# A fused attention and two-MLP kernel: scores of k by halves, attention spread over the batch before, idle-time products, float narrowing shifted to ScalarE

## The chip, the cores and the metric

One Trainium2 chip, one core. The metric is the device time of one execution in microseconds, the median of several runs. In the profile PE is TensorE's matrix products, PEld its weight loads, DVE VectorE, ACT ScalarE, POOL GpSimd and SP SyncE, whose queue issues nearly all transfers.

## The reference

For 8 batches with 8 heads, 576 tokens and 64 features per head, 32 packing queries p per head gather the sequence, and the tokens q read the gathered result; the heads then form rows of 512 for two MLPs:

```python
p_packed = softmax(p @ k.T / 8) @ v          # 32 x 64 per head
out = softmax(q @ p_packed.T / 8) @ p_packed # 576 x 64 per head
x = out.transpose(0, 2, 1, 3).reshape(4608, 512)
h = x @ w_in                                 # 512 x 2048
x = where(h > 0, h, exp(min(h, 0)) - 1) @ w_out
h = x @ w_in2                                # 512 x 1024
solu = h * softmax(h)
ln = (solu - mean(solu)) / sqrt(var(solu) + 1e-6) * g_ln
out = ln @ w_out2
```

q, k, v and p come as 4-byte floats, the four weight matrices as 8-byte floats.

## The kernel before

**Narrowing.** The weights arrive as pairs of 32-bit words and are made 4-byte floats in 48 units of 128 x 512 (`narrow`, L94): 32 for the first MLP (`wi`, `wo`), 16 for the second (`wi2`, `wo2`). Per unit ScalarE scales the high word as a float (L105), VectorE shifts it left by 3 (L107), ORs in the low word shifted right by 29 (L109) and ORs in the sign (L113). Planner names: cvA, cvS, cvO, cvG.

**Exact products.** Every big product takes three passes over a high and a low part of each operand (`mm3`, L64 to L66). The second product of attention is folded into w_in: M = p_packed times a 64-row block of w_in (`m_mm`), four chunks c per batch, so the first MLP's h comes straight from the attention weights AT and M.

**Attention of a batch.** Two groups g of four heads run one after the other: `s1_mm` forms the scores of k with p laid out as block diagonals (`pt_bd`, zeros elsewhere), 8 instructions of 128 rows by 64 columns; maximum, exponential and division (`s1_max`, `s1_exp`, `s1_div`); a transpose, in batches 0 and 1 on TensorE (`t1_mm`), from batch 2 on by VectorE's 32 x 32 blocks and 16 copies into `a_sb` (`t1_blocks`, `t1_move`, L295); then `pp_mm` multiplies by v and `pp_blocks` (L319) or `pp_t` puts the result, transposed, into `ppT`. Then two halves of 288 tokens: `s2_mm` (scores of q, 16 instructions of 64 rows by 32 columns through `packed_mm`, L332), softmax over blocks of 32 on VectorE, with the exponential on ScalarE (`s2_tr` to `s2_back`, L349 to L377), and a split into AT.

**FFN steps.** 256 steps (batch, half, f), each 6 products for h (L64 to L66), two activations on ScalarE (L418, L419), a maximum on VectorE (L424), a cast (L431) and a subtraction (L434), and, three steps behind, 12 products into the accumulators. The first three halves are done by quarters of f, so that not all weights are needed at once.

**PSUM.** Eight banks: two double ones "acc", one double one "misc" (scores, transposes, pp, M, in turn), two for h.

**The order.** A planner, `order`, emits all nodes of the first part on TensorE, VectorE, ScalarE and SP. A node has an engine, an estimated time, what it needs, the buffers that it takes and frees, and perhaps a due time; of the nodes that can start within 0.3 us on an engine the one with the earliest latest start is emitted. FFN step n is due at `FIRST_US + STEP_US * n` (30.0 and 2.79); attention nodes have no due time of their own, only what follows from their users. `first` is the order of the first transfers on SP's queue; p of batch 0 goes by ScalarE's queue in two pieces, after `pt_bd` is cleared. The last part (`solu_ln` to `out_mm`), the second MLP, follows in an order written out by hand.

Of the kernel before, what the change touches and what calls it, by code (L numbers as in the profile page):

```python
# [34 lines left out]
def attention_mlp_kernel(ctx: ExitStack, tc: tile.TileContext, q, k, v, v_tail, p,  # L35
# [58 lines left out]
    def narrow(raw, name, dst=None):  # L94
# [125 lines left out]
    def load_v(b, g, tag=None):  # L220
        if tag is None:
            t = v_sb
        else:
# [4 lines left out]
        vt[b, g] = t

    def load_q(b, half, tag=None):  # L230
        if tag is None:
            t = work.tile([P, 4, HS], F32, tag="q", name=f"q{b}_{half}", bufs=1)
        else:
            t = slot(f"q{b}_{half}", [P, 4, 512], tag, F32)[:, :, 0:HS]
        sp.dma_start(out=t, in_=q[b, half])
        qt[b, half] = t

    def s1_mm(b, g, ps2=misc_ps):
        o = ps2(f"s1_{b}_{g}")
        kk = kt.pop((b, g))  # L240
        for kh in range(2):
            for j in range(2):
                pe.matmul(o[64 * j:64 * j + 64, kh, 0:HS], pt_bd[:, 2 * g + j, :],
                          kk[:, j, kh * HS:(kh + 1) * HS], start=True, stop=True)
        st["s1", g] = o

    def s1_max(b, g):
        nm = small.tile([P, 1], F32, tag="nm", name=f"nm{b}_{g}")
        dve.tensor_reduce(out=nm, in_=st["s1", g][:, :, 0:HS], axis=AX.XY, op=ALU.max, negate=True)
        dve.tensor_scalar(out=nm, in0=nm, scalar1=0.125, scalar2=None, op0=ALU.mult)  # L250
        st["nm", g] = nm

    def s1_exp(b, g):
        e = work.tile([P, S], F32, tag="at", name=f"e1_{b}_{g}", bufs=3)
        sm = small.tile([P, 1], F32, tag="sm", name=f"sm{b}_{g}")
        act.activation(e.rearrange("p (a c) -> p a c", a=2), st.pop(("s1", g))[:, :, 0:HS], AF.Exp,
                       scale=0.125, bias=st.pop(("nm", g)), accum_out=sm)
        st["e1", g] = e, sm

    def s1_div(b, g):  # L260
        e, sm = st["e1", g]
        r = small.tile([P, 1], F32, tag="r", name=f"r{b}_{g}")
        dve.tensor_scalar(out=sm, in0=sm, scalar1=1e-9, scalar2=None, op0=ALU.add)
        dve.reciprocal(r, sm)
        dve.tensor_scalar(out=e, in0=e, scalar1=r, scalar2=None, op0=ALU.mult)

    def t1_mm(b, g, ps2=misc_ps):
        e, _ = st.pop(("e1", g))
        o = ps2(f"t1_{b}_{g}")
# [3 lines left out]
        st["t1", g] = o  # L273

    def t1_a(b, g):
        act.copy(a_sb[:, 0:4].rearrange("p c n -> p (c n)"), st["t1", g][:, 0])

    def t1_b(b, g):
        dve.tensor_copy(a_sb[0:S - 4 * CH, 4], st["t1", g][0:S - 4 * CH, 1, 0:P])

    def t1_blocks(b, g):
        e, _ = st.pop(("e1", g))
        t = work.tile([P, S], F32, tag="at", name=f"eB{b}_{g}", bufs=3)
        dve.transpose(t, e)
        st["eB", g] = t.rearrange("p (c n) -> p c n", n=NP)

    def t1_move(b, g, h, eng):
        t = st["eB", g]
        for j in range(4):
            n = len(range(j, S // NP, 4))  # L290
            x, y = a_sb[j * NP:(j + 1) * NP, 0:n, h * NP:(h + 1) * NP], t[h * NP:(h + 1) * NP, j::4]
            if eng is act:
                act.copy(x, y)
            else:
                dve.tensor_copy(x, y)  # L295

    def pp_mm(b, g, ps2=misc_ps):


        o = ps2(f"pp{b}_{g}")  # L300
        vv = vt.pop((b, g))
        for u in range(2 if b < 2 else 0):
            for c in range(5):
# [731 lines left out]
```

## Time and profile before

| | |
|---|---|
| median of 3 runs | 1182.26 us (1179.63 to 1182.43) |
| the profiled execution | 1178.58 us, of which the span is 1176.8 us |
| TensorE busy | 1117.9 us (95%) |
| VectorE busy | 894.4 us (76%) |
| ScalarE busy | 718.6 us (61%) |
| GpSimd busy | 21.3 us (2%) |
| mean granted clock of TensorE | 0.987 |

Busy shares are averages over the whole span; the kernel has an opening, a stretch in which weights are narrowed beside the first steps, a long steady stretch, and the second MLP. Matrix products are pipelined, so their durations overlap, and the distance between two starts tells the rate. A line can belong to a helper.

### The profile page before, as it was taken

Reading aid. Unit: us, or ns where it says so; the run is one execution under the profiler, and the core shown is the slowest. Engines: PE = TensorE matmul, PEld = TensorE weight load, DVE = VectorE, ACT = ScalarE, POOL = GpSimd, SP = SyncE. Lnnn points to the kernel's source line nnn. Section 1 sums busy time; section 2 is a strip of 40 time slices with the busy share of each in tenths; the row PEclk is TensorE's granted clock in tenths of the full one; section 3 lists DMA queues with packets and bytes.
Section 4 is the critical chain, followed back from the end, with each engine's and each line's share of the span. In section 5 each row is a group of like instructions: output and inputs, shape, how many; then the busy total and the mean of one; then the engine's idle time right before and its main releaser. Section 6 shows DMA issues by size and latency. Waiting matters only on the chain.

```text
span 1176.8 us, 20606 instructions
## 1 busy us (share of the span) xinstructions
PE 1117.9 (95%) x7916; PEld 979.5 (83%) x7916; DVE 894.4 (76%) x2022; ACT 718.6 (61%) x1539; POOL 21.3 (2%) x45
## 2 busy tenths in 40 slices
PE   4699999899999999999999999999999999999997
PEld 2478889699799899899889889988888888888885
DVE  4999995858858868767877765478888788788774
ACT  2567765465465565565466465647766766766674
POOL 0000000000000000000000000000000000000000
PEclk7799999999999999999999999999999999999999
DMA  9837332213322412321422151611111111000000
GB/s 328 333 117 235 121 111 82 84 41 113 101 93 72 145 57 97 119 93 62 132 80 90 46 178 59 218 57 54 54 37 54 52 39 54 27 28 19 28 28 36
DMA packets 53554, 111.04 MB, mean 94 GB/s; under 512 B 8400, under 2 KB 27600, under 8 KB 51664
## 3 DMA queue, kind: packets, MB, share of 16 engines
q1 hardware_dynamic: 52912, 109.66, 27.5%
q8 instruction: 62, 1.02, 0.4%
q14 instruction: 36, 0.29, 0.1%
q10 hardware_dynamic: 544, 0.07, 0.0%
HBM read 77.14 MB, written 32.57 MB: 93 GB/s over the span
## 4 chain that ended last, share of the span: by engine, by line
PE 42%; DVE 31%; ACT 14%; issue 7%; DMA 4%; POOL 1%; SPq 0%; ACTq 0%; POOLq 0%; DVEq 0%
PE acc L64 8%; PE acc L66 8%; PE acc L65 8%; ACT lnX L542 6%; PE h L64 5%; PE h L65 5%; PE h L66 4%; DVE lnB L532 4%; DVE a_sb L295 2%; DVE ln L525 2%; PE m L332 2%; DVE z L517 2%; ACT h L520 2%; DVE lnT L151 2%; DVE nm L508 2%
## 5 line engine op out<-in xcount | busy, mean ns | idle before, releaser
L64 PE MATMUL acc<-ghi,wo 128*128 128x288 f32 x1024 | 308.6, 301 | 1.7 <-ACT x L471 0.7
L66 PE MATMUL acc<-glo,wo 128*128 128x288 f32 x1024 | 302.7, 296 | 1.4 <-DVE glo L434 1.4
L65 PE MATMUL acc<-ghi,wo 128*128 128x288 f32 x1024 | 302.2, 295 | 0.0
L64 PEld LDWEIGHTS acc<-ghi,wo 128*128 128x128 f32 x1024 | 191.9, 187 | 30.8 <-ACT fe L419 14.8
L66 PEld LDWEIGHTS acc<-glo,wo 128*128 128x128 f32 x1024 | 192.6, 188 | 2.6 <-DVE glo L434 2.0
L65 PEld LDWEIGHTS acc<-ghi,wo 128*128 128x128 f32 x1024 | 192.6, 188 | 0.0
L559 PE MATMUL o<-wo,lnT 128*128 128x512 f32 (+1 forms) x592 | 185.5, 386 | 5.6 <-ACT lnT L149 5.6
L424 DVE SCALAR_TENSOR_TENSOR fe<-fe,h 128x288 f32<-128x288 f32 x256 | 114.3, 452 | 88.6 <-ACT fe L419 86.0
L418 ACT ACTIVATE fe<-h 128x288 f32<-128x288 f32 x256 | 104.5, 408 | 118.2 <-PE h L66 92.8
L431 ACT CAST ghi<-fe 128x288 fp32r<-128x288 f32 x256 | 109.4, 431 | 105.2 <-DVE fe L424 104.4
L64 PE MATMUL h<-AT,M 128*128 128x288 f32 x512 | 156.0, 305 | 9.7 <-DVE fe L424 8.9
L542 ACT COPY lnX<-lnB 32x256 f32<-32x256 f32 x288 | 116.3, 404 | 78.0 <-DVE lnB L532 65.2
L65 PE MATMUL h<-AT,M 128*128 128x288 f32 x512 | 152.4, 298 | 0.9 <-DVE M L400 0.9
L66 PE MATMUL h<-AT,M 128*128 128x288 f32 x512 | 150.8, 294 | 0.0
L434 DVE TENSOR_TENSOR glo<-fe,ghi 128x288 fp32r<-128x288 f32 x256 | 114.5, 452 | 46.4 <-ACT ghi L431 42.8
L559 PEld LDWEIGHTS o<-wo,lnT 128*128 128x128 f32 x592 | 111.3, 190 | 28.3 <-ACT lnT L149 6.5
L64 PEld LDWEIGHTS h<-AT,M 128*128 128x128 f32 x512 | 96.6, 189 | 27.5 <-DVE fe L424 11.4
L419 ACT ACTIVATE fe<-fe 128x288 f32<-128x288 f32 x256 | 113.8, 445 | 8.0
L561 PE MATMUL o<-wo,lnT 128*128 128x512 f32 (+1 forms) x296 | 113.9, 386 | 0.0
L64 PE MATMUL h<-wi,x2hi 128*128 128x512 f32 x288 | 112.3, 390 | 1.4 <-ACT h L520 1.4
L65 PE MATMUL h<-wi,x2lo 128*128 128x512 f32 x288 | 112.1, 389 | 0.0
L66 PE MATMUL h<-wi,x2hi 128*128 128x512 f32 x288 | 112.0, 389 | 0.0
(98 smaller groups left out, 1581.8 us busy)
## 6 DMA issues: line engine op xcount, KB each, us to landing
k<-in_k SPq DMA_DIRECT2D x16, 576.0 KB, 3.9
q<-in_q SPq DMA_DIRECT2D x16, 576.0 KB, 3.9
x_dram<-x SPq DMA_DIRECT2D x32, 288.0 KB, 2.5
x2raw<-x_dram SPq DMA_DIRECT2D x9, 1024.0 KB, 5.5
out_x<-y SPq DMA_DIRECT2D x35, 256.0 KB, 2.0
raw_wi<-in_w_in SPq DMA_DIRECT2D x8, 1024.0 KB, 9.3
w_dram<-w SPq DMA_DIRECT2D x16, 512.0 KB, 2.7
v_sb<-in_v SPq DMA_DIRECT2D x14, 512.0 KB, 3.9
```

The lines of the kernel that those rows point to most:

```text
L64: pe.matmul(o, a[0], b[0], start=start, stop=False)
L65: pe.matmul(o, a[1], b[0], start=False, stop=False)
L66: pe.matmul(o, a[0], b[1], start=False, stop=stop)
L418: act.activation(e, o[:, 0:HS], AF.Relu, scale=-1.0)
L419: act.activation(e, e, AF.Exp, scale=-1.0)
L424: dve.scalar_tensor_tensor(out=e, in0=e, scalar=-1.0, in1=o[:, 0:HS], op0=ALU.add, op1=ALU.max)
L431: act.copy(ghi, e)
L434: dve.tensor_tensor(out=glo, in0=e, in1=ghi.bitcast(F32), op=ALU.subtract)
L532: dve.transpose(t, last.pop(("ln", i)))
L542: act.copy(x, y)
L559: pe.matmul(o, t[:, x, kk], w[:, 0, cs], start=x + kk == 0, stop=x == 1 and kk == 7)
L561: pe.matmul(o, t[:, 0, kk], w[:, 1, cs], start=False, stop=False)
```

## The change

In `narrow` the left shift moves into the first OR, and the top three bits of the low word are made as an integer by a ScalarE activation, in place (cvL in the place of cvS). The scores of k come in two halves w of 288 tokens for all eight heads, with p undoubled (`p_sb`) and the same product form as the scores of q (`heads_mm`, which is `packed_mm` with the weights as an argument); the two halves' maxima, sums and factors are joined (`s1_both`, `s1_scale`, `s1_fac`). `a_sb` holds both halves r of the heads, and one pp group of a batch follows for both. k, q and v share three single buffers of one size from batch 2 on, and v has no zero rows any more. Attention nodes from batch 2 on get due times (`by`) within the 32 steps of the batch before. The first transfers are reordered, p first on SP's queue. Where the planner sees TensorE idle ahead of the first h, products of a tile of ones are issued into a spare h bank, which nobody reads. Lines of the old code that go, printed above, are mostly left out here.

```diff
--- before.py
+++ after.py
@@ -100,14 +100,16 @@
...
         act.activation(t.bitcast(F32), raw[:, :, 1].bitcast(F32), AF.Copy, scale=2.0 ** -111)
         yield
-        dve.tensor_scalar(out=t, in0=t, scalar1=3, scalar2=None, op0=ALU.logical_shift_left)
+        act.activation(raw[:, :, 0], raw[:, :, 0], AF.Identity, scale=2.0 ** -29 * (1 - 2.0 ** -10), bias=under)
         yield
-        dve.scalar_tensor_tensor(out=t, in0=raw[:, :, 0], scalar=29, in1=t,
-                                 op0=ALU.logical_shift_right, op1=ALU.bitwise_or)
+        dve.scalar_tensor_tensor(out=t, in0=t, scalar=3, in1=raw[:, :, 0],
+                                 op0=ALU.logical_shift_left, op1=ALU.bitwise_or)
...
+    under = const.tile([P, 1], F32, name="under")
...
-    pt_bd = const.tile([P, 4, 2 * NP], F32, name="pt_bd")
-    a_sb = const.tile([P, 5, P], F32, name="a_sb")
-    v_sb = const.tile([P, 5, 4 * D], F32, name="v_sb")
+    p_sb = const.tile([P, 4, NP], F32, name="p_sb")
+    a_sb = const.tile([P, 5, 2, P], F32, name="a_sb")
...
+    def room_for(name, tag):
+        if tag in ("k", "q", "v"):
+            return work.tile([P, 5 * 4 * D], F32, tag=tag, name=name, bufs=1)
+        return slot(name, [P, 2048], tag, F32)
+    def load_p(b):
+        sp.dma_start(out=p_sb, in_=p[b])
+    def load_k(b, half, tag):
+        t = room_for(f"k{b}_{half}", tag)[:, 0:4 * HS].rearrange("p (u t) -> p u t", u=4)
+        for g in range(2):
+            sp.dma_start(out=t[:, 2 * g:2 * g + 2], in_=k[b, g][:, :, half * HS:(half + 1) * HS])
+        kt[b, half] = t
+    def load_v(b, g, tag):
+        t = room_for(f"v{b}_{g}", tag)[:, 0:20 * D].rearrange("p (c d) -> p c d", c=5)
+        sp.dma_start(out=t[:, 0:4], in_=v[b, g])
...
+    def load_q(b, half, tag):
+        t = room_for(f"q{b}_{half}", tag)[:, 0:4 * HS].rearrange("p (u t) -> p u t", u=4)
...
+    def s1_mm(b, w, ps2=misc_ps):
+        o = st["s1", w] = ps2(f"s1_{b}_{w}")
+        heads_mm(o[:, :, 0:HS], p_sb, kt.pop((b, w)))
...
+        dve.tensor_reduce(out=nm, in_=st["s1", w][:, :, 0:HS], axis=AX.X, op=ALU.max, negate=True)
...
+    def s1_exp(b, w, r):
+        if w == 0:
+            st["e1", r] = work.tile([P, S], F32, tag="at", name=f"e1_{b}_{r}", bufs=3)
+        act.activation(st["e1", r][:, w * HS:(w + 1) * HS], st["s1", w][:, r, 0:HS], AF.Exp, scale=0.125,
+                       bias=st["nm"][:, w, r:r + 1], accum_out=st["sm"][:, w, r:r + 1])
+    def s1_both(b):
+        nm = st["nm"]
+        m = small.tile([P, 1, 2], F32, tag="m1", name=f"m1_{b}")
+        dve.tensor_tensor(out=m, in0=nm[:, 0:1], in1=nm[:, 1:2], op=ALU.min)
+        dve.tensor_tensor(out=nm, in0=m.to_broadcast([P, 2, 2]), in1=nm, op=ALU.subtract)
+    def s1_scale(b):
+        nm = st["nm"]
+        act.activation(nm, nm, AF.Exp)
+    def s1_fac(b):
+        f, sm = st.pop("nm"), st.pop("sm")
+        dve.tensor_tensor(out=sm, in0=f, in1=sm, op=ALU.mult)
+        r = small.tile([P, 1, 2], F32, tag="r1", name=f"r1_{b}")
+        dve.scalar_tensor_tensor(out=r, in0=sm[:, 0:1], scalar=1e-9, in1=sm[:, 1:2], op0=ALU.add, op1=ALU.add)
+        dve.reciprocal(r, r)
+        dve.tensor_tensor(out=f, in0=f, in1=r.to_broadcast([P, 2, 2]), op=ALU.mult)
+        st["f"] = f
+    def s1_div(b, r):
+        e = st["e1", r]
+        for w in range(2):
+            x = e[:, w * HS:(w + 1) * HS]
+            dve.tensor_scalar(out=x, in0=x, scalar1=st["f"][:, w, r:r + 1], scalar2=None, op0=ALU.mult)
...
+    def t1_move(b, r, u, js):
+        t = st["eB", r]
+        for j in js:
...
+            dve.tensor_copy(a_sb[j * NP:(j + 1) * NP, 0:n, r, u * NP:(u + 1) * NP], t[u * NP:(u + 1) * NP, j::4])
+    def pp_mm(b, ps2=misc_ps):
+        o = st["pp"] = ps2(f"pp{b}")
...
+        for c in range(5):
...
+            for u1 in range(2):
+                for h in range(4):
+                    u, r = 2 * (h // 2) + u1, h % 2
+                    vv = vt[b, u // 2]
+                    d0 = (2 * (u % 2) + r) * D
+                    pe.matmul(o[h * NP:(h + 1) * NP, u1, 0:D], a_sb[0:n, c, r, u * NP:(u + 1) * NP],
+                              vv[0:n, c, d0:d0 + D], start=(c == 0), stop=(c == 4))
+    def pp_copy(b):
+        dve.tensor_copy(pp_t2[b % 2].rearrange("p u n -> p (u n)"), st["pp"][:, 0, 0:P])
+    def pp_blocks(b, h):
+        o, t = st["pp"], pp_t2[b % 2]
+        u0, r = 2 * (h // 2), h % 2
+        for x in range(2):
+            n0 = r * D + x * NP
+            dve.transpose(t[n0:n0 + NP, u0:u0 + 2, :], o[h * NP:(h + 1) * NP, :, x * NP:(x + 1) * NP])
+    def heads_mm(o, w, x):
...
+                pe.matmul(o[u * NP:(u + 1) * NP, r], w[rows, u, :], x[rows, u, :], start=True, stop=True)
...
+                (("cvL", *key), ACT, 0.66, [], {}),
...
     def attn_nodes(b):
+        def by(step):
+            return dict(due=FIRST_US + STEP_US * (32 * (b - 1) + step)) if b > 1 else {}
...
+            k_tag, v_tag, q_tag = ("k", "M0"), ("v", "M1"), ("q", "M2")
...
+            k_tag, v_tag, q_tag = ("k", "M1"), ("v", "M2"), ("q", "k")
...
+            k_tag, v_tag, q_tag = ("k", "q"), ("v", "k"), ("q", "k")
...
+        if b:
+            node(("p", b), SP, 0.4, [("s1", b - 1, 1)], lambda: load_p(b), size=0.1)
+        for w in range(2):
+            node(("k", b, w), SP, 0.8, [], lambda w=w: load_k(b, w, k_tag[w]), takes=[kp[w]], size=0.6)
+        for w in range(2):
+            acc = b == 0 and w == 1
+            bank = ("acc" if acc else "misc", ("s1", b, w))
+            node(("s1", b, w), PE, 0.85,
+                 [("p", b) if b else None, ("k", b, w), ("s1", b, 0) if w else None, *early],
+                 lambda w=w, acc=acc: s1_mm(b, w, acc_ps if acc else misc_ps), takes=[bank, *([] if w else es)], lets=[kp[w]],
+                 **by(2.5 + 4 * w))
+            node(("max", b, w), DVE, 0.93, [("s1", b, w), ("max", b, 0) if w else None], lambda w=w: s1_max(b, w))
+            for r in range(2):
+                node(("exp", b, w, r), ACT, 0.63, [("max", b, w), ("exp", b, 0, r) if w else None],
+                     lambda w=w, r=r: s1_exp(b, w, r), lets=[bank])
...
+            node(("v", b, g), SP, 0.8, [], lambda g=g: load_v(b, g, v_tag[g]), takes=[vp[g]], size=0.6)
+        node(("both", b), DVE, 0.25, [("exp", b, w, r) for w in range(2) for r in range(2)], lambda: s1_both(b))
+        node(("fexp", b), ACT, 0.2, [("both", b)], lambda: s1_scale(b))
+        node(("fac", b), DVE, 0.65, [("fexp", b)], lambda: s1_fac(b))
+        prev_pp = ("pp", b - 1) if b else None
+        a_in = []
+        for r in range(2):
+            node(("div", b, r), DVE, 0.6, [("fac", b)], lambda r=r: s1_div(b, r))
...
+                eb = ("at", ("eB", b, r))
+                node(("eB", b, r), DVE, 0.77, [("div", b, r)], lambda r=r: t1_blocks(b, r), takes=[eb], lets=[es[r]],
+                     **by(9 + 4 * r))
+                a_in += [node(("mv", b, r, u, j), DVE, 0.5, [("eB", b, r), prev_pp],
+                              lambda r=r, u=u, j=j: t1_move(b, r, u, (j, j + 1)), lets=[eb],
+                              **by(10 + 4 * r + u + j / 4))
+                         for u in range(4) for j in (0, 2)]
+        bank = ("acc" if b == 0 else "misc", ("pp", b))
+        node(("pp", b), PE, 2.4 if b < 2 else 1.8, a_in + [("v", b, g) for g in range(2)], lambda: pp_mm(b, acc_ps if b == 0 else misc_ps),
+             takes=[bank], lets=vp, **by(18))
+        if b < 2:
+            node(("ppt", b, 0), DVE, 0.3, [("pp", b)], lambda: pp_copy(b), lets=[bank])
+        else:
+            for h in range(4):
+                node(("ppt", b, h), DVE, 0.5, [("pp", b)], lambda h=h: pp_blocks(b, h), lets=[bank],
+                     **by(18.6 + 0.4 * h))
+        ppt = ppt_of(b)
...
+            qp = (q_tag[half], ("q", *x))
+            node(("q", *x), SP, 0.4, [], lambda half=half: load_q(b, half, q_tag[half]), takes=[qp], size=0.6)
...
+            node(("s2", *x), PE, 1.0, [*ppt, ("q", *x),
...
+                 takes=[bank, u], lets=[qp], **by(20.5 + 4 * half))
...
+            prev = node(("back", *x), DVE, 0.77, [prev], lambda half=half: s2_back(b, half), takes=[a], lets=[u],
+                        **by(24.5 + 4 * half))
...
+        node(("m", *x), PE, 1.35, [*ppt_of(b), *(("cvG", "wi", c, u) for u in range(4))],
+             lambda: m_mm(b, c), takes=[bank, mp], lets=[(f"wi{c}", c)] if b == B - 1 else [],
+             due=FIRST_US + STEP_US * (32 * (b - 1) + (27, 30, 33, 36.5)[c]) if b > 1 else None)
...
+        node(("fm", *x), DVE, 0.45, [("fx", *x)], lambda: ffn_max(b, half, f), lets=[hp], due=due + 2 * STEP_US)
...
+                        dict(lets=[accs_of[i]], takes=[] if again else [xos[i]], due=due + STEP_US * AHEAD)),
...
+    first = [("k", 0, 0), ("k", 0, 1), *raw("wi", 0, 0, 1), ("v", 0, 0), ("v", 0, 1), ("q", 0, 0), ("q", 0, 1),
+             *raw("wo", 0, 0), ("p", 1), ("k", 1, 0), *raw("wo", 1, 0), *raw("wi", 1, 0, 1), ("k", 1, 1), ("v", 1, 0), ("v", 1, 1),
+             ("q", 1, 0), *raw("wo", 2, 0), *raw("wo", 3, 0, 1), *raw("wi", 2, 0, 1)]
...
+            if v["eng"] == PE:
+                idle = t - max(free[PE], FILL_FROM)
+                if idle > 0 and not any(y[0] == "h" for y in end):
+                    result.append(int(FILL_PART * idle / 0.22))
...
+    FILL_FROM, FILL_PART = 0.4, 0.75
+    ones = const.tile([P, P], F32, name="ones")
+    dve.memset(ones, 1.0)
+    spare = h_ps("spare")
+    load_p(0)
...
+    dve.memset(under, -0.5 + 7.5 * 2.0 ** -10)
...
+            if isinstance(x, int):
+                for _ in range(x):
+                    pe.matmul(spare[:, 0:P], ones, ones, start=True, stop=True)
+            else:
+                nodes[x]["emit"]()
...
```

## Rows read from the trace of the kernel before

**Rows 1.** Busy time by stretch: length, each engine's busy time (instructions), clock, DMA share, GB/s.

```profile
0.00:37.00 37.00, 15.21 (x155) 8.81 (x155) 19.19 (x43) 10.00 (x18) 1.56 (x9) 0.72 0.93 331
37.00:60.00 23.00, 18.23 (x150) 14.24 (x150) 21.58 (x49) 14.78 (x32) 0.00 (x0) 0.85 0.79 312
60.00:180.00 120.00, 115.46 (x933) 104.29 (x930) 110.45 (x222) 82.14 (x183) 0.00 (x0) 1.00 0.46 147
180.00:747.00 567.00, 551.02 (x4767) 502.64 (x4766) 411.36 (x1008) 325.65 (x741) 0.00 (x0) 1.00 0.28 92
```

**Rows 2.** The same stretches, the first activation of each FFN step (L418) alone.

```profile
60.00:180.00 120.00, 17.43 (x43) 1.00 0.46 147
180.00:747.00 567.00, 81.79 (x200) 1.00 0.28 92
```

**Rows 3.** Timeline of the opening: start, length, engine, line, operation, idle before.

```profile
9.87 3.69 PE L243 MATMUL s<-k,pt_bd 128*64 128x288 f32 x16 [9.87 <-DMA pt_bd<-in_p]
...
23.73 1.57 PE L332 MATMUL s<-q,ppT 64*32 64x288 f32 x16
...
34.15 1.96 PE L332 MATMUL m<-wi,ppT 64*32 64x512 f32 x16 [6.35 <-DVE u L349]
...
36.85 0.61 PE L64 MATMUL h<-AT,M 128*128 128x288 f32 x1 [0.75 <-ACT M L396]
```

**Rows 4.** A stretch of the opening, TensorE and its granted clock alone.

```profile
15.90:43.00 27.10, 16.19 (x153) 0.51 0.98 360
```

**Rows 5.** A stretch, the shift that is removed (L107) alone.

```profile
60.00:180.00 120.00, 9.29 (x22) 1.00 0.46 147
```

**Rows 6.** Groups by line and shape: count, busy us, mean ns.

```profile
L109 DVE SCALAR_TENSOR_TENSOR cv_wi<-raw_wi,cv_wi 128x512 uint32<-128x512 uint32 x24 | 16.4, 687 | 0.3
...
L105 ACT ACTIVATE cv_wi<-raw_wi 128x512 f32<-128x512 f32 x24 | 15.8, 674 | 7.0 <-DVE wi L113 6.3 <-DMA raw_wi<-in_w_in 0.8
...
L256 ACT ACTIVATE e<-s,nm 128x576 f32<-128x576 f32 x16 | 11.8, 740 | 16.8 <-DVE nm L250 16.8
L362 ACT ACTIVATE u<-u 128x576 f32<-128x576 f32 x16 | 10.9, 684 | 11.2 <-DVE u L358 11.1
...
L107 DVE TENSOR_SCALAR cv_wi<-cv_wi 128x512 uint32<-128x512 uint32 x24 | 10.2, 430 | 1.9 <-ACT cv_wi L105 0.9
...
L319 DVE STREAM_TRANSPOSE ppT<-pp 32x32 f32<-32x32 f32 x96 | 20.3, 212 | 1.2
...
L256 ACT ACTIVATION_READ_ACCUMULATOR e<-s,nm 128x1 f32 x16 | 3.1, 193 | 0.0
```

**Rows 7.** Timeline of TensorE in the steady stretch, around the scores of q and k.

```profile
538.72 0.29 PE L66 MATMUL acc<-glo,wo 128*128 128x288 f32 x1
538.94 0.71 PE L332 MATMUL s<-q,ppT 64*32 64x288 f32 x16
...
539.83 0.29 PE L65 MATMUL h<-AT,M 128*128 128x288 f32 x1
539.96 0.29 PE L66 MATMUL h<-AT,M 128*128 128x288 f32 x1
...
545.11 0.29 PE L66 MATMUL h<-AT,M 128*128 128x288 f32 x1
545.33 1.19 PE L243 MATMUL s<-k,pt_bd 128*64 128x288 f32 x8
...
546.68 0.30 PE L65 MATMUL acc<-ghi,wo 128*128 128x288 f32 x1
```

**Rows 8.** TensorE's waits, 180 to 747 us: total, times, longest.

```profile
PE h L64 <- DVE fe L424: 5.3, 6, 1.0
PE pp L310 <- PE h L66: 3.5, 5, 0.7
```

**Rows 9.** Two early stretches by all engines; DMA share and GB/s stand last.

```profile
2.50:9.50 7.00, 0.00 (x0) 0.00 (x0) 0.00 (x0) 1.48 (x2) 0.00 (x0) 1.00 0.95 311
9.50:50.00 40.50, 24.85 (x200) 15.35 (x200) 31.04 (x67) 16.44 (x33) 0.31 (x1) 0.66 0.99 378
```

More of the change, by code (lines that the diff above doesn't have):

```diff
@@ L260, in s1_div @@
[L260 to L269, printed above, removed]
+    def s1_mm(b, w, ps2=misc_ps):
+        o = st["s1", w] = ps2(f"s1_{b}_{w}")
+        heads_mm(o[:, :, 0:HS], p_sb, kt.pop((b, w)))
@@ L272, in t1_mm, with t1_a @@
             pe.transpose(o[0:n, c // 4, c % 4 * P:(c % 4 + 1) * P], e[:, c * CH:c * CH + n], ident)
[L273 to L283, printed above, removed]
+    def t1_a(b, r):
+        act.copy(a_sb[:, 0:4, r], st["t1", r][:, 0].rearrange("p (c n) -> p c n", c=4))
@@ L284, in t1_blocks, with t1_b @@
+    def t1_b(b, r):
+        dve.tensor_copy(a_sb[0:S - 4 * CH, 4, r], st["t1", r][0:S - 4 * CH, 1, 0:P])
+    def t1_blocks(b, r):
+        e = st.pop(("e1", r))
+        t = work.tile([P, S], F32, tag="at", name=f"eB{b}_{r}", bufs=3)
         dve.transpose(t, e)
[L285 to L289, printed above, removed]
+        st["eB", r] = t.rearrange("p (c n) -> p c n", n=NP)
+    def t1_move(b, r, u, js):
+        t = st["eB", r]
+        for j in js:
@@ L303, in pp_mm @@
+    def pp_mm(b, ps2=misc_ps):
+        o = st["pp"] = ps2(f"pp{b}")
+        for u in range(4 if b < 2 else 0):
             for c in range(5):
+                n = min(CH, S - c * CH)
                 for r in range(2):
-                    h = 2 * u + r
-                    pe.matmul(o[r * D:(r + 1) * D, 0, u * NP:(u + 1) * NP], vv[:, c, h * D:(h + 1) * D],
-                              a_sb[:, c, h * NP:(h + 1) * NP], start=(c == 0), stop=(c == 4))
-        for c in range(0 if b < 2 else 5):
-            for h in range(4):
-                pe.matmul(o[h * NP:(h + 1) * NP, 0, 0:D], a_sb[:, c, h * NP:(h + 1) * NP],
-                          vv[:, c, h * D:(h + 1) * D], start=(c == 0), stop=(c == 4))
@@ new lines, in attn_nodes @@
+            k_tag, v_tag, q_tag = ("k", "q"), ("v", "k"), ("q", "k")
+        early = [("back", b - 1, 1)] if b else []
+        kp = [(k_tag[w], ("k", b, w)) for w in range(2)]
+        vp = [(v_tag[g], ("v", b, g)) for g in range(2)]
+        es = [("at", ("e", b, r)) for r in range(2)]
+        if b:
+            node(("p", b), SP, 0.4, [("s1", b - 1, 1)], lambda: load_p(b), size=0.1)
+        for w in range(2):
+            node(("k", b, w), SP, 0.8, [], lambda w=w: load_k(b, w, k_tag[w]), takes=[kp[w]], size=0.6)
@@ L764, in step_nodes @@
                       [(("xe", *x, i), eng, 0.72, [("x2", *x), ("part", *run) if again else None],
-                        dict(lets=[accs_of[i]], takes=[] if again else [xos[i]], due=due + STEP_US * (AHEAD + 1))),
+                        dict(lets=[accs_of[i]], takes=[] if again else [xos[i]], due=due + STEP_US * AHEAD)),
                        (("xout", *x, i), SP, 0.4, [], dict(lets=[xos[i]], size=0.3))])
```

147 lines of the change are left out of this document (25 added, 122 removed).

## Prediction

> **What bounds the kernel now.** I read the busy time by stretch first, because the average hides four different stages. The last 430 of 1176.8 us (from 747 us on) are the second MLP, which the change leaves alone but for the width of two buffers, so I compare only what lies before. From 180 to 747 us TensorE is busy 551.0 of 567 us and VectorE 411 [rows 1]: TensorE is the bound, and only its own work or its 16 us of gaps can shorten this stretch. From 60 to 180 us TensorE has 115.5 of 120 us and VectorE 110.5: a double bound. From 37 to 60 us VectorE has 21.6 of 23 us and TensorE 18.2: VectorE is the bound, and TensorE's clock is still low for part of it (mean 0.85). Up to 37 us nothing is full but the DMA share, at 0.93 [rows 1].
>
> The count of FFN steps agrees: 43 steps in 120 us (2.79 us each), then 200 in 567 us (2.84 us each) [rows 2]. The pace hardly changes after 60 us, so the real loss of the first stage lies ahead of that: the first product of a step starts at 36.85 us [rows 3].
>
> The opening's timeline shows why. The first scores wait until 9.87 us for p, which comes in two small transfers on ScalarE's queue. The scores of q start at 23.73 us, since both groups of four head pairs run scores, transposes and products one after the other; the second half of these scores holds the only two "misc" banks until VectorE has transposed it, and so the first M comes only at 34.15, after 6.35 us of idle TensorE [rows 3]. The granted clock from 15.9 to 43 us is 0.51, the lower of its two levels, with 10.9 of the 27.1 us idle [rows 4].
>
> **The change, part by part.** *Narrowing.* Each of 48 units loses one VectorE instruction of 0.430 us (the group shown has 24, its twin for w_out 24) [rows 6]. The shift moves into the OR that stays, priced at its present 0.687 us: same two operands, one more operation. Total 48 x 0.43 = 20.6 us of VectorE: 32 units are of the first MLP, 22 of them between 60 and 180 us [rows 5], so 10 ahead of that, 4 of which (w_in's first chunk) must precede the first h; the second MLP's 16 come later. ScalarE gains one activation a unit. Its nearest row is the other strided one, 0.674 us. It also reads a bias per partition: k's exponential, with a bias, takes 0.740 and q's, without, 0.684 for the same 576 columns, so 0.73 us; upper bound twice 0.674, as it also writes with a stride [rows 6]. In 60 to 180 us that puts 22 x 0.73 = 16 us onto 82 [rows 1]: 98 of 120, covered; at the upper bound 112, no longer covered.
>
> The Trainium skill speaks against this edit: "ScalarE: Activation LUTs", section "Rules for kernel authors", wants multiplies and adds on VectorE, and by the same page's figures an activation with a pointer bias on 512 columns would be an estimated 0.71 us. Going by that rule alone the edit loses 0.3 us of engine time a unit, 13 us over 48; the stretch rows say the engine that gives is the bound and the one that takes is not.
>
> *Scores of k.* Before, a batch has two groups of 8 products with 128 rows by 64 columns; afterwards two halves of 16 with 64 by 32, exactly the form that q's scores have today. In the steady stretch consecutive 288-column products start 0.13 us apart (539.83, 539.96). Around q's scores two such steps take 539.83 - 538.72 = 1.11 us, so these cost 1.11 - 0.27 = 0.84; around k's, 546.68 - 545.11 = 1.57, so 1.30 [rows 7]. Six batches (2 to 7) run in the steady stretch, 12 calls x 0.46 = 5.5 us off the bound. Bounds: nothing, if p's weights behave otherwise, to 6.
>
> *Softmax of k by halves.* ScalarE: four exponentials of 288 columns for two of 576, each with its own accumulator read (0.193), plus one tiny one: about +1 us a batch; VectorE: two more tiny instructions and shorter scalings, about +0.7. pp's block transposes go from 16 of 0.212 to 8 of double width, -1.5 us [rows 6]. Over a batch of 32 x 2.84 = 91 us VectorE and ScalarE have a quarter and two fifths free [rows 1], so all this is priced at nothing; uncovered it would be under 1 us a batch.
>
> *One pp group.* The same 40 products a batch, one entry and exit instead of two, and all copies into a_sb wait only for the previous batch's pp. Changes of shape cost: between the last full product and k's scores, the start gap is 0.22 instead of 0.13 [rows 7]. The last chunk now has 64 rows instead of 128 padded with zeros, which is one more change. "TensorEngine Tiling (Array Packing)", section "Key Properties", of the Trainium skill says that changing the tiling mode drains the engine; by it the 64-row chunk would give back what the missing group saves, and the row of k's scores agrees in kind (0.09 us). I take -1 us in all, bounds -2 to +1.
>
> *Attention spread.* From batch 2 on, attention nodes get due times across the preceding batch. Two stalls recur there: h waiting for the FFN's VectorE result (5.3 us in six waits) and pp starting late behind h (3.5 us in five) [rows 8]. I take back a quarter, -2 us; bounds -8.8 (all) to a loss, see the rivals.
>
> *The opening.* p goes first on SP's queue, k is loaded by halves, and w_in comes ahead of v. p and half of k are 0.66 MB; the stretch from 2.5 us moves 311 GB/s [rows 9], so they land about 5 us, and scores start near 6 instead of 9.87. Then the queue rate decides: k, p and w_in's first 2.1 MB make 3.3 MB, 2.2 of them by 9.5 us and the rest at 378 GB/s by 12.6; v's 1.2 MB by 15.7; the first half of q (0.6 MB) by 17.3 [rows 9]. So pp cannot start before about 16, and its 80 instructions and copy end near 20: q's scores near 20.5, 3 us earlier. The four narrowings, which now sit between the first FFN inputs on VectorE, fit in the gap from 13 to 20. From q's scores to the first h there remain six passes of about 0.76 and short ones on VectorE, two on ScalarE: about 8.5 us. First h near 29.5, so 7 us earlier; bounds 3 (only q's scores move) to 9.
>
> *Unread products.* They stand where the planner sees TensorE idle, at 75% of the gap. Where the gap is real they cost nothing; if the planner is early, at most their own surplus, under 2 us at the start, inside the bound of 3. What they buy: q's scores take 1.57 us at the low clock against 0.71 [rows 3, 7], and everything up to 43 us runs like that [rows 4]. In 37 to 60 us this, with the other six early units off VectorE (2.6 us of 21.6), is worth 2.5 us; VectorE sets it. From 60 to 180 us VectorE loses 22 x 0.43 = 9.5 of 110.5 us, but TensorE has only 4.5 us of gaps to give [rows 1]; I take 1.5.
>
> Sum: -(7 + 2.5 + 1.5) - 5.5 - 1 - 2 = -19.5 us. The profiled execution took 1178.6 us, so 1159.1; the median of the three runs is 3.7 higher, their lowest 1.0 higher. I predict 1161 us.
>
> **The rivals.** *The opening's advance is given back (17%).* k's second half and v of batch 1 now come behind w_in's next 2.1 MB, 5.6 us at 378 GB/s, and ScalarE has two activations in every narrowing. If batch 1 is late for step 8, or the 112 us bound holds, only about 2.5 of the 11 us stay: 1178.6 - 2.5 - 8.5 + 2 = 1170. Against it: ScalarE has 18% left at my price.
>
> *More than forecast (10%).* With VectorE relieved, all gaps from 60 to 747 us close (20.5 us [rows 1]) instead of 3.5 us of them; less the 3.5, and half of the other 17, 8.5, gives 1152.
>
> *Slower (11%).* The due times put attention ahead of the FFN's own chain: activation, maximum, cast, subtraction on ScalarE and VectorE between h and the products three steps behind. Two h buffers cover it today but for one wait of 1.0 us a batch [rows 8]. The 32 copies into a_sb, in 8 nodes per half of the heads, stand in that queue. It decides at 19.5 / 6 = 3.3 us of added h waits a batch, 0.1 us in every step; half as much again gives 1180.6 + 9.8 = 1190.
>
> *No change to speak of (5%).* Gains and such waits cancel, 1176 to 1184.
>
> **How the numbers follow.** The forecast has 57%, 1154 to 1168. Two runs of this kernel differ by up to 2.8 us, so under 0.3% (3.5 us) nothing can be told. Faster: 57 + 17 + 10 = 84%; same 5%; slower 11%. The range that leaves out no more than 2 in 10 runs from the better rival to the worse one with its margin: 1148 to 1176.
>
> **What would show it.** In the profile after: first h near 29 to 30 us; granted clock near 1 from some 8 us on; k's scores costing about 0.84 us between neighbours; VectorE's total some 20 us lower, ScalarE's some 40 higher; the steady stretch about 8 us shorter at the same number of steps. Wrong if h waits grow by more than 3 us a batch, if ScalarE passes 90% before 180 us, or if the first h stays behind 33 us.

## The result, and the profile after

| | before | after |
|---|---|---|
| median of 4 runs | 1180.95 us (1179.58 to 1182.43) | 1146.26 us (1142.79 to 1148.46) |
| ratio to before, 95% interval | | 0.970 [0.967, 0.973] |
| the profiled execution; its span | 1178.58; 1176.8 us | 1142.79; 1141.0 us |

The change saves 34.7 us. The forecast was 1161 us with a range down to 1148: right in direction, 15 us short in size. The page of the kernel after, its busy line and the TensorE clock in 40 slices:

```profile
PE 1114.4 (98%) x8164; PEld 984.1 (86%) x8164; DVE 868.5 (76%) x1956; ACT 750.7 (66%) x1627; POOL 20.4 (2%) x42
...
PEclk9899999999999999999999999999999999999999
```

VectorE's total fell by 25.9 us and ScalarE's rose by 32.1, about as predicted (20 and 40). TensorE's busy time, 15.9 us of the unread products now among it, fell by 3.5 us while its share rose from 95 to 98%. Without those products it fell by 19.4 of the 35.8 us that the span lost: about half of the gain is busy time, and about half is idle time. By stretch, with the columns of [rows 1], then the first activation of each step (L433 now), as in [rows 2]:

```profile
0.00:37.00 37.00, 29.03 (x318) 22.65 (x318) 24.09 (x53) 17.86 (x36) 0.70 (x6) 0.92 0.96 348
37.00:60.00 23.00, 20.74 (x221) 16.60 (x222) 20.07 (x47) 17.77 (x42) 0.00 (x0) 0.90 0.87 336
60.00:180.00 120.00, 114.49 (x917) 104.44 (x916) 111.20 (x240) 95.58 (x211) 0.00 (x0) 1.00 0.49 154
180.00:747.00 567.00, 564.29 (x5000) 521.19 (x4999) 400.73 (x953) 351.11 (x813) 0.56 (x1) 1.00 0.30 100
```

```profile
60.00:180.00 120.00, 17.04 (x42) 1.00 0.49 154
180.00:747.00 567.00, 84.77 (x207) 1.00 0.30 100
```

From 180 to 747 us TensorE's gaps went from 16.0 us [rows 1] to 2.7, and 207 steps start where 200 did: 2.74 us a step instead of 2.84. From 60 to 180 us one step fewer starts, and VectorE is as full as before (111.2 of 120 us) although it lost the shift: other work has moved in there. ScalarE stands at 95.6 of 120, near the predicted 98.

The opening, as in [rows 3]:

```profile
1.05 4.50 PE L1020 MATMUL spare<-ones 128*128 128x128 f32 x26 [1.05 <-DVE under L1012]
5.49 0.71 PE L348 MATMUL s<-k,p_sb 64*32 64x288 f32 x16
...
8.24 3.62 PE L1020 MATMUL spare<-ones 128*128 128x128 f32 x30
...
20.26 0.72 PE L348 MATMUL s<-q,ppT 64*32 64x288 f32 x16 [0.20 <-DVE ppT L332]
...
26.87 0.72 PE L348 MATMUL s<-q,ppT 64*32 64x288 f32 x16
...
29.48 0.40 PE L64 MATMUL h<-AT,M 128*128 128x288 f32 x1 [1.47 <-ACT AT L152]
...
37.70 0.61 PE L64 MATMUL h<-AT,M 128*128 128x288 f32 x1 [4.25 <-DVE fe L439]
```

Scores of k start at 5.49 us (forecast 6), those of q at 20.26 (20.5), the first h at 29.48 (29.5), 7.4 us earlier. The profile is that of the fastest of the four executions; e6, e7 and e10 below, with the same opening, start their first h at 30.17 to 31.40. The last line is what the forecast had not: after the first products TensorE stands for 4.25 us, waiting for the FFN's maximum.

The steady stretch around k's scores, as in [rows 7], and around the pp group:

```profile
315.11 0.29 PE L66 MATMUL acc<-glo,wo 128*128 128x288 f32 x1
315.33 0.72 PE L348 MATMUL s<-k,p_sb 64*32 64x288 f32 x16
...
316.21 0.29 PE L65 MATMUL h<-AT,M 128*128 128x288 f32 x1
...
353.94 0.29 PE L66 MATMUL acc<-glo,wo 128*128 128x288 f32 x1
354.17 1.46 PE L328 MATMUL pp<-v,a_sb 128*32 128x64 f32 x80
...
355.79 0.30 PE L65 MATMUL h<-AT,M 128*128 128x288 f32 x1
```

k's scores cost 316.21 - 315.11 - 0.27 = 0.83 us instead of 1.30, pp 355.79 - 353.94 - 0.27 = 1.58 us a batch. TensorE's waits from 180 to 747 us, as in [rows 8], are down to two: the maximum's, from 5.3 us to 1.6, and one later; pp no longer waits.

```profile
PE h L64 <- DVE fe L439: 1.6, 1, 1.6
PE h L64 <- ACT h L535: 0.8, 1, 0.8
```

**Where the time came from.** The number of a step is the same in every kernel, so the time at which a step's first activation starts on ScalarE says how far a kernel is. After, steps 0, 48, 80 and 255:

```profile
31.11 0.41 ACT L433 ACTIVATE fe<-h 128x288 f32<-128x288 f32 x1 [1.68 <-PE h L66]
...
177.74 0.41 ACT L433 ACTIVATE fe<-h 128x288 f32<-128x288 f32 x1 [0.61 <-PE h L66]
...
263.99 0.41 ACT L433 ACTIVATE fe<-h 128x288 f32<-128x288 f32 x1
...
738.01 0.41 ACT L433 ACTIVATE fe<-h 128x288 f32<-128x288 f32 x1 [3.58 <-PE h L66]
```

The same for all kernels on which the argument rests; the last three columns are differences (us):

| kernel | step 0 | 0 to 48 | 48 to 80 | 80 to 255 |
|---|---|---|---|---|
| before | 39.67 | 143.32 | 94.84 | 494.86 |
| after | 31.11 | 146.63 | 86.25 | 474.02 |
| before, new narrowing alone | 39.90 | 142.52 | 90.52 | 499.47 |
| before, spread alone | 40.07 | 157.15 | 88.46 | 480.46 |
| before, spread and new narrowing | 38.49 | 145.51 | 88.43 | 479.86 |
| after, old narrowing | 32.27 | 160.35 | 86.66 | 473.22 |
| after, no unread products | 36.36 | 147.79 | 86.24 | 477.18 |

Step 0 comes 8.6 us earlier, of which 3.3 are lost again by step 48; steps 48 to 80 give 8.6 and steps 80 to 255 give 20.8. Step 48 stands near 180 us, where the forecast parted its stages: ahead of it the forecast 11 us came to 5.3, behind it the forecast 8.5 us came to 29.4. Each row is one execution. The kernels of the second and the last row run the same instructions in the same order but for the unread products, and still differ by 3.2 us between steps 80 and 255.

### The profile page after: what moved, and what is told of

The parts are those of the page before. It is cut to its first block, busy times and chain, and to the rows that moved or that the text cites. A ratio compares the mean times of both kernels' runs of the same rounds, so it can differ in the third digit from the quotient of the medians.

```text
span 1141.0 us, 21041 instructions
## 1 busy us (share of the span) xinstructions
PE 1114.4 (98%) x8164; PEld 984.1 (86%) x8164; DVE 868.5 (76%) x1956; ACT 750.7 (66%) x1627; POOL 20.4 (2%) x42
## 4 chain that ended last, share of the span: by engine, by line
PE 54%; DVE 22%; ACT 15%; issue 6%; POOL 1%; DMA 1%; POOLq 0%; SPq 0%; ACTq 0%; DVEq 0%
PE acc L64 11%; PE acc L66 10%; PE acc L65 10%; ACT lnX L557 6%; PE h L64 6%; PE h L66 6%; PE h L65 6%; DVE lnB L547 4%; PE m L348 3%; DVE ln L540 2%; DVE z L532 2%; ACT h L535 2%; DVE lnT L154 2%; DVE nm L523 2%; PE s L348 2%
## 5 line engine op out<-in xcount | busy, mean ns | idle before, releaser
L64 PE MATMUL h<-AT,M 128*128 128x288 f32 x512 | 155.7, 304 | 10.6 <-DVE fe L439 9.0
L433 ACT ACTIVATE fe<-h 128x288 f32<-128x288 f32 x256 | 104.7, 409 | 91.3 <-PE h L66 85.9
```

The lines of the kernel that those rows point to most:

```text
L64: pe.matmul(o, a[0], b[0], start=start, stop=False)
L433: act.activation(e, o[:, 0:HS], AF.Relu, scale=-1.0)
```

## The experiments

Twelve kernels, each timed in three rounds beside the kernel before. Numbers are the median and the ratio to before with its 95% interval. The interval reaches up to 4.5 us to either side where the kernel's runs spread most, so ratios that differ by less are read together with a row of the trace.

**e1: no new due times at all.**

```diff
         def by(step):
-            return dict(due=FIRST_US + STEP_US * (32 * (b - 1) + step)) if b > 1 else {}
+            return {}
...
-             due=FIRST_US + STEP_US * (32 * (b - 1) + (27, 30, 33, 36.5)[c]) if b > 1 else None)
+             due=None)
...
-  lambda: ffn_max(b, half, f), lets=[hp], due=due + 2 * STEP_US)
+  lambda: ffn_max(b, half, f), lets=[hp])
...
-  takes=[] if again else [xos[i]], due=due + STEP_US * AHEAD)),
+  takes=[] if again else [xos[i]], due=due + STEP_US * (AHEAD + 1))),
```

> The changed kernel without the due times: attention nodes, M, the maximum and the accumulator copy fall back to the due times of before. Theory A (the steady stretch gained mainly because the spread attention no longer stalls TensorE): about 12 us slower than the changed kernel, near 1158 us, with a stall of about 1 us between accumulator and h products once a batch again. Theory B (the gain comes from the shapes: k's scores and one pp group): at most 4 us slower, near 1149 us.

Measured: 1213.77 us, 1.026 [1.023, 1.029]: 67 us lost, and 32 us slower than before. All theories were too small. Its waits of TensorE from 180 to 747 us, and a piece of its timeline:

```profile
PE pp L328 <- DVE a_sb L306: 47.4, 23, 3.6
```

```profile
401.51 0.27 PE L328 MATMUL pp<-v,a_sb 128*32 128x64 f32 x2 [2.78 <-DVE a_sb L306]
...
405.28 0.43 PE L328 MATMUL pp<-v,a_sb 128*32 128x64 f32 x4 [3.50 <-DVE a_sb L306]
```

pp is emitted where the planner believes its copies done; on the chip it stands at the head of TensorE's queue, computes what has been copied, and waits for the next copy with every FFN product behind it. One group for all heads needs all copies at once, and without due times it stood waiting for them; whether two groups would have waited less in the changed kernel was not tried.

The waits are not all of the loss. With each of six such stalls the granted clock falls to 0.50, the lower of its two levels, and stays there for 10 to 14 us, in which full products start 0.24 us apart instead of 0.13:

```profile
404.00:414.20 10.20, 6.78 (x93) 5.97 (x94) 8.04 (x31) 2.08 (x5) 0.00 (x0) 0.50 0.25 82
```

From 180 to 747 us the clock's mean is 0.94; in the kernel after it is 1.00.

**e8: the due times of the attention nodes alone gone.**

```diff
         def by(step):
-            return dict(due=FIRST_US + STEP_US * (32 * (b - 1) + step)) if b > 1 else {}
+            return {}
```

> The changed kernel without the due times of the attention nodes (copies, pp, scores, transposes); M and the FFN keep theirs. If the 67 us lost without any due times come from pp standing in TensorE's queue ahead of its copies: near 1210 us, 9 us of waits before pp a batch. Rival, they come from the FFN's due times: near 1150 us.

Measured: 1197.20 us, 1.013 [1.010, 1.017]: 51 of the 67 us, largely by the same wait, with a mean clock of 0.96 from 180 to 747 us:

```profile
PE pp L328 <- DVE a_sb L306: 33.4, 17, 3.6
```

**e11: of the attention's due times those of the copies alone** (eB and mv).

```diff
+        def copies_by(step):
+            return dict(due=FIRST_US + STEP_US * (32 * (b - 1) + step)) if b > 1 else {}
         def by(step):
-            return dict(due=FIRST_US + STEP_US * (32 * (b - 1) + step)) if b > 1 else {}
+            return {}
...
-                     **by(9 + 4 * r))
+                     **copies_by(9 + 4 * r))
...
-                              **by(10 + 4 * r + u + j / 4))
+                              **copies_by(10 + 4 * r + u + j / 4))
```

> The changed kernel with due times in attention for the block transposes and copies into a_sb alone. If pp stood in the queue because its copies had no priority on VectorE: most of the 51 us without attention due times comes back, near 1152 us, no wait before pp. Rival, pp's own place in the queue matters too: 1165 us or more.

Measured: 1176.91 us, 0.996 [0.995, 0.998]: 20 of the 51 us come back. pp's wait is out of the list, but others are longer than in the kernel before or new:

```profile
PE h L64 <- DVE fe L439: 13.9, 6, 3.3
PE s L348 <- PE h L66: 4.6, 5, 1.0
```

So getting the copies done early enough is one part, and the places of pp, of the scores and of what hangs on them are the other.

**e7: old due times of the FFN's maximum and accumulator copy**, the last two edits of e1.

```diff
-  lambda: ffn_max(b, half, f), lets=[hp], due=due + 2 * STEP_US)
+  lambda: ffn_max(b, half, f), lets=[hp])
...
```

> The changed kernel with the old due times of the FFN's maximum and accumulator copy; attention keeps its due times. Theory C (the maximum's own due time removed the wait of h for it, 1.15 us a batch): 7 us slower, near 1153 us, with that wait back in every batch. Theory D (spreading attention removed it): within 2 us of the changed kernel.

Measured: 1147.05 us, 0.971 [0.968, 0.974]: nothing. It is not the maximum's own due time that shortened the waits for it; with attention's places taken away they were back at 13.9 us (e11).

**e9: the kernel before, with due times alone**: beside the lines shown, pp at 10 + 8g, its transposes at 10.6 + 8g, s2 at 20.5 + 4 half, back at 24.5 + 4 half, and M as in the change.

```diff
+        def by(step):
+            return dict(due=FIRST_US + STEP_US * (32 * (b - 1) + step)) if b > 1 else {}
...
-                 lets=[kp])
+                 lets=[kp], **by(1 + 8 * g))
...
-                     takes=[("at", ("eB", *x))], lets=[("at", ("e", *x))])
+                     takes=[("at", ("eB", *x))], lets=[("at", ("e", *x))], **by(4.5 + 8 * g))
...
-                             lets=[("at", ("eB", *x))]) for h in range(4)]
+                             lets=[("at", ("eB", *x))], **by(5 + 8 * g + h)) for h in range(4)]
...
```

> The kernel before with due times for its own attention nodes from batch 2 on (two groups, old narrowing, old shapes): group g's scores 1 + 8 g steps into the batch before, its copies from 5 + 8 g, pp at 10 + 8 g, q's scores and M as in the changed kernel. Theory A (spreading alone takes the waits out of the steady stretch, about 2 us a batch): 10 to 12 us faster than before, near 1171 us. Theory E (due times only mend what the single pp group would break, the old kernel gains nothing by them): within 3 us of before, near 1180 us.

Measured: 1169.82 us, 0.990 [0.989, 0.992]: 11.3 us by the ratio, where the forecast had 2. The table shows a loss behind it: steps 48 to 255 gain 20.8 us, of the 29.4 in the kernel after, but steps 0 to 48 take 13.8 us longer. Busy time from 140 to 180 us in the kernel before, then in this one two stretches:

```profile
140.00:180.00 40.00, 38.70 (x300) 35.92 (x299) 36.28 (x74) 27.39 (x63) 0.00 (x0) 1.00 0.35 110
```

```profile
140.00:180.00 40.00, 33.09 (x242) 28.39 (x241) 38.06 (x87) 22.45 (x49) 0.00 (x0) 0.96 0.31 90
180.00:747.00 567.00, 563.68 (x4890) 519.53 (x4889) 410.31 (x1003) 332.14 (x763) 0.00 (x0) 1.00 0.30 97
```

Batch 2's attention now lies beside the narrowing; there VectorE has 38.1 of 40 us and TensorE only 33.1.

**e4: the kernel before, with the new narrowing alone.**

```diff
-        dve.tensor_scalar(out=t, in0=t, scalar1=3, scalar2=None, op0=ALU.logical_shift_left)
+        act.activation(raw[:, :, 0], raw[:, :, 0], AF.Identity, scale=2.0 ** -29 * (1 - 2.0 ** -10), bias=under)
...
-                (("cvS", *key), DVE, 0.42, [], {}),
+                (("cvL", *key), ACT, 0.66, [], {}),
```

> The kernel before with the new narrowing alone. By the prediction's terms 4 us faster than before, near 1177 us. Rival, what VectorE gives ScalarE takes: within 2 us of before, near 1181 us.

Measured: 1176.76 us, 0.996 [0.995, 0.997]: 4.8 us. In its profiled execution step 80 comes 4.9 us earlier, but steps 80 to 255 take 4.6 us longer, so the profile doesn't show where the medians' gain is kept.

**e12: the two together**, the edits of e9 and of e4.

> The kernel before with the due times of the spread run and the new narrowing together, nothing else changed. Theory F (due times crowd the first stage until VectorE bounds it, and then its 13.8 us of relief count in full): 13 us faster than the spread alone, near 1157 us, step 48 back by some 13 us. Theory G (the two add as they stand alone, 11.3 and 4.8 us): near 1165 us.

Measured: 1157.43 us, 0.979 [0.978, 0.981]: 24.3 us, of which the narrowing has 13.0 on top of the spread's 11.3. The stretch from 140 us:

```profile
140.00:180.00 40.00, 38.48 (x336) 35.44 (x336) 37.57 (x89) 28.94 (x65) 0.00 (x0) 1.00 0.41 121
```

VectorE is as busy as in e9, but TensorE has 5.4 us more of work in it, and steps 0 to 48 take 145.51 us instead of 157.15. In these steps VectorE is busy 144.4 us in e9, 134.5 here and 135.2 in the kernel after, 92% of the time in all three; what is taken off it shortens the stage. In the kernel before it has 91% (130.9 us), but TensorE has 94%, and the narrowing alone gave only 0.8 us there (e4).

**e2: the change with the old narrowing**, e4's edit the other way round: both shifts on VectorE.

> The changed kernel with the old narrowing (both shifts on VectorE). If VectorE's relief counts as in the prediction (2.6 us up to 60 us, 1.5 us up to 180 us), 4 us slower, near 1150 us. Rival, ScalarE has become the tighter engine between 60 and 140 us (70.9 of 80 us busy): no slower, or faster, 1142 to 1147 us.

Measured: 1159.22 us, 0.981 [0.979, 0.983]: 13 us lost, 13.7 of them between steps 0 and 48. 27 of the first MLP's 32 shifts fall into these steps, 27 x 0.43 = 11.6 us, and VectorE is busy 145.2 us in them instead of 135.2. So the shifts count in full, in the stage where VectorE is the bound; the 2 us beyond them were not traced.

**e3: no unread products.**

```diff
-    FILL_FROM, FILL_PART = 0.4, 0.75
+    FILL_FROM, FILL_PART = 0.4, 0.0
```

> The changed kernel without the unread products (share of the gap 0 in place of 0.75). If the clock in the opening counts: first h 1 to 2 us later, 2 to 4 us slower, near 1149 us. Rival, the opening is set by transfers and VectorE: within 1 us of the changed kernel, near 1146 us.

Measured: 1151.53 us, 0.974 [0.971, 0.977]: 4 to 5 us lost. The opening by stretch and timeline:

```profile
0.00:37.00 37.00, 19.93 (x180) 11.02 (x181) 19.74 (x45) 15.15 (x31) 0.70 (x6) 0.67 0.95 348
```

```profile
30.77 1.22 PE L348 MATMUL s<-q,ppT 64*32 64x288 f32 x16 [2.87 <-issue]
...
34.20 0.61 PE L64 MATMUL h<-AT,M 128*128 128x288 f32 x1 [2.22 <-ACT AT L152]
```

Without them the mean granted clock up to 37 us is 0.67 instead of 0.92, the second half of q's scores takes 1.22 us instead of 0.72 (26.87 in the opening after), and the first h comes at 34.20 instead of 29.48. Between these two profiles that is nearly two thirds of the opening's 7.4 us. The start of k's scores varies from run to run; counted from it, the way to the first h takes 29.6 us here and 23.7 to 24.6 in the kernel after, e6, e7 and e10. The lengths of products are the surer sign than the clock column: that reads 1.00 up to 37 us in e9, whose first scores of q take 1.57 us as in the kernel before [rows 3].

**e5: the change with the old shape of k's scores**, four products of 128 rows by 64 columns a half, with ones as weights.

```diff
-        heads_mm(o[:, :, 0:HS], p_sb, kt.pop((b, w)))
+        kk = kt.pop((b, w))
+        for u in range(4):
+            pe.matmul(o[64 * (u % 2):64 * (u % 2) + 64, u // 2, 0:HS], ones[:, 0:64], kk[:, u, :],
+                      start=True, stop=True)
```

> The changed kernel with k's scores in the old shape: 4 products of 128 rows by 64 columns a half in place of 8 of 64 by 32, with a tile of ones as weights, so the scores are not those of p. Theory A (the shape is worth what the distances of starts say, 0.56 us a call in the steady stretch, 12 calls): 6.8 us slower than the changed kernel, near 1153 us. Theory B (the saving came from the order, not the shape): at most 2 us slower, below 1149 us.

Measured: 1150.57 us, 0.975 [0.971, 0.979]: 5.4 us by the ratio, 4.3 by the medians. The timeline gives the same without their spread:

```profile
318.93 0.29 PE L66 MATMUL acc<-glo,wo 128*128 128x288 f32 x1
319.15 1.19 PE L241 MATMUL s<-k,ones 128*64 128x288 f32 x8
...
320.51 0.29 PE L65 MATMUL h<-AT,M 128*128 128x288 f32 x1
```

320.51 - 318.93 - 0.27 = 1.31 us against 0.83, and 12 x 0.48 = 5.8.

**e6: pp of batches 2 to 7 in two groups again**, the second a step later.

```diff
+            node(("pp0", b), PE, 1.0, a_in + [("v", b, g) for g in range(2)], lambda: pp_mm(b, misc_ps, (0,)),
+                 takes=[bank], **by(17.5))
+            node(("pp", b), PE, 1.0, [("pp0", b), ("h", *steps[32 * (b - 1) + 18][:3])], lambda: pp_mm(b, misc_ps, (1,)),
+                 lets=vp, **by(18))
...
```

> The changed kernel with the pp products of batches 2 to 7 in two groups of 20, an FFN step between them. If each entry costs what it did before (1.16 us a group of 20 against 1.48 for one of 40): 0.84 us a batch, 5 us in all, near 1151 us. Rival, the entry is hidden: within 1.5 us of the changed kernel.

Measured: 1149.30 us, 0.972 [0.969, 0.976]: 2.2 us by the ratio, not to be told from the change by its interval. Each group of 40 costs 1.02 us between its neighbours' starts (357.83 - 356.54 - 0.27), so going back to two costs 2 x 1.02 - 1.58 = 0.46 us a batch, 2.8 us in six:

```profile
356.54 0.29 PE L66 MATMUL h<-AT,M 128*128 128x288 f32 x1
356.76 0.90 PE L330 MATMUL pp<-v,a_sb 128*32 128x64 f32 x40
...
357.83 0.30 PE L65 MATMUL acc<-ghi,wo 128*128 128x288 f32 x1
```

That is more than the term forecast at 1, because each of these groups ends in a 64-row chunk of its own. The kernel before, with 128 rows throughout, has groups that nothing delays:

```profile
302.35 0.29 PE L66 MATMUL h<-AT,M 128*128 128x288 f32 x1
302.57 0.77 PE L310 MATMUL pp<-v_sb,a_sb 128*32 128x64 f32 x40
...
303.50 0.30 PE L65 MATMUL acc<-ghi,wo 128*128 128x288 f32 x1
```

They cost 303.50 - 302.35 - 0.27 = 0.88 us, so the term itself is 2 x 0.88 - 1.58 = 0.18 us a batch, 1.1 us in six.

**e10: batch 2's due times pressed into its later steps**, so that its attention would leave the first stage.

```diff
         def by(step):
+            if b == 2:
+                step = 10 + 0.75 * step
```

> The changed kernel with the due times of batch 2 alone moved later (10 + 0.75 of the step), so that its attention leaves the crowded stretch ahead of step 48. If the opening's advance is given back to that early attention: step 48 some 3 us earlier, and 2 to 4 us faster than the changed kernel, near 1143 us. Rival, the work is only moved: within 1.5 us, near 1146 us.

Measured: 1145.07 us, 0.970 [0.967, 0.974]: no change, and step 48 starts at 178.83 us, 1.1 later. What still holds the first 48 steps at 3.05 us each (146.63 / 48) is left open; moving batch 2's due times by some steps doesn't help it.

## Why the prediction was wrong in size

By these pairs the change divides up as follows (ratio differences times 1181 us): spread 11.3, narrowing on top of it 13.0, unread products 4.3, shape of k's scores 5.4. With 1.1 for the one pp group, by the distances under e6, that is 35 us, against 35.1 for the change by its own ratio. This would leave about nothing for the rest, the reordered opening with its transfers above all, which had no run of its own. The parts come from different starting points, so the sum is a plausibility, not a proof.

**Two steps failed.**

*"I take back a quarter, -2 us"* (attention spread). Alone it was worth 11.3 us, past the bound of 8.8, and behind step 48, where the term was meant, 20.8 (e9). The bound was called "all", but it held only the two stalls that recur [rows 8]. The other five lines of that view are these:

```profile
PE pp L310 <- DVE ppT L319: 3.1, 1, 3.1
PE s L332 <- issue: 1.3, 4, 0.5
PE s L332 <- DVE ppT L319: 1.2, 1, 1.2
PE m L332 <- DVE M L400: 1.0, 3, 0.4
PE acc L66 <- DVE glo L434: 0.5, 1, 0.5
```

All seven make 15.9 us, the 16 us that TensorE's busy time leaves free in this stretch [rows 1]; that row was in my hands, and I used it only for a rival of 10%. And even that is too little. I added up the distances between TensorE's starts over steps 64 to 160, less the 0.133 us pitch of each full product: 14.1 us a batch before, 9.8 after. Of these 4.3 us the shapes (e5, e6) account for 2 x 0.48 + 0.18 = 1.1, and 3.1 are order, 17 us over the 5.5 batches from step 80 to 255; e9, by order alone, gains 14.4 in the same steps. After the change the four scores of a batch at 0.84, its four M at 1.21 and its pp at 1.58 make up the whole 9.8, so order has next to nothing left to give here. Ends of products are modelled, so a product that starts late by less than its modelled length leaves no gap; the distances of starts show it. The rival "slower" by due times had the mechanism upside down for the steady stretch: without due times the merged pp stalls TensorE (e1, e8). Ahead of step 48 it was right in kind: there the spread cost 13.8 us with the old narrowing (e9).

*"VectorE loses 22 x 0.43 = 9.5 of 110.5 us, but TensorE has only 4.5 us of gaps to give; I take 1.5"* (60 to 180 us). I costed the narrowing on the stage as it was before, while another part of the same change refilled that stage. Alone, the narrowing gave 4.8 us (e4), close to the 4 that the forecast gave it in all. With batch 2's attention moved in front of step 48, VectorE sets the pace there (e9), and the shifts count for 13 (e2, e12). The two parts had to be costed together: the spread takes 13.8 us from the first 48 steps (143.32 to 157.15), and the narrowing gives 11.6 of them back (145.51).

The Trainium skill's rule that speaks against the edit ("ScalarE: Activation LUTs", section "Rules for kernel authors": adds and multiplies on VectorE) goes by the price of an element, and in price the trace agrees: ScalarE paid 0.761 us a unit for the added activation, to spare VectorE 0.430. As advice on where to put the work it does not hold here, as e2 shows the kernel 13 us faster for the dearer form: which engine bounds the stage decides, not which does an element faster.

**What was right.** The opening's three times, each within about 0.5 us in the profile shown. That is in part luck: nearly two thirds of the gain went with the unread products (e3), which the forecast counted only from 37 us on. k's scores cost 0.83 us for a forecast 0.84, 5.4 us in all for a forecast 5.5. The one pp group gave 1.1 us for a forecast 1. Its 64-row chunk costs 1.02 - 0.88 = 0.14 us, and the entry that it saves is worth 2 x 0.88 + 0.14 - 1.58 = 0.32. The Trainium skill states that a change of tiling mode drains TensorE ("TensorEngine Tiling (Array Packing)", section "Key Properties"); both figures agree in kind, but the chunk gives back less than half of what the missing group saves, and not all of it, as I had read the rule. ScalarE's cover held: even at 70.9 of 80 us from 60 to 140 us it is not the bound, as e2, which relieves it, is slower.

```profile
60.00:140.00 80.00, 76.44 (x633) 68.52 (x632) 74.55 (x151) 70.89 (x155) 0.00 (x0) 1.00 0.53 172
```

**The rivals.** "More than forecast" came nearest in mechanism (TensorE's gaps close) and still forecast 6 us too much time. "The opening's advance is given back" happened in part: 3.3 of 8.6 us were lost by step 48. The spread by itself explains this much: with the new narrowing it lengthens those steps by 3.0 us in the kernel before, whose opening is the old one (142.52 to 145.51). Whether a late transfer takes part as well wasn't separated. The range should have reached to the sum of the two stages with all gaps closed, plus the term of the shapes; I had let the gaps stand for half.

## What to carry to other kernels

Bound what a better order can give by the distances of starts on the engine that sets the pace, not by the stalls that recur in the list of waits: those held 8.8 us, all its idle time 16, and 20.8 were to be had (e9). Where one part of a change moves work into another stage, cost the other parts on the stage as it will then be: an instruction taken off VectorE was worth 4.8 us in 48 units before the move and 13 after it. A merged group that needs all its inputs at once needs a place in the queue at which they are certainly there: without attention's due times this kernel lost 51 us, part of it by the lower clock behind each stall, and 20 came back with the due times of the copies alone.

## What the runs showed of the hardware

The in-place activation on strided integers took 0.761 us for 128 x 512, against 0.674 for the strided float one of [rows 6] and the forecast 0.73:

```profile
L109 ACT ACTIVATE raw_wi<-raw_wi,under 128x512 uint32<-128x512 uint32 x24 | 17.8, 761 | 0.0
L111 DVE SCALAR_TENSOR_TENSOR cv_wi<-cv_wi,raw_wi 128x512 uint32<-128x512 uint32 x24 | 16.4, 689 | 4.0 <-ACT raw_wi L109 3.8
```

The OR that took over the shift costs what it did before (0.689 against 0.687).

The first products ran slowly: the first 26 unread ones took 4.50 us, 0.17 each, a later 30 took 3.62, 0.12 each. And the clock was lost again after the opening: from 29.5 to 43 us, the stretch with the 4.25 us wait for the maximum, the granted clock has a mean of 0.62, with TensorE busy 8.8 of 13.5 us.

```profile
29.50:43.00 13.50, 8.76 (x64) 6.00 (x65) 13.15 (x26) 8.48 (x21) 0.00 (x0) 0.62 1.03 377
```

VectorE has 13.15 of those 13.5 us, so there too it is VectorE that leaves TensorE idle. Whether taking more narrowing off it there (the sign's OR on GpSimd, say) would close this was not tried.
